# Three networks in one kernel: the last network's weights rebuilt from head 14 on, three of them as float16 pairs, and spatial weights 2.4 heads later

## The chip, the cores and the metric

The kernel runs on one core of a Trainium2 chip. Its metric is the device time in microseconds (us) of one execution; before the change it is 740.44 us, the median of three runs (739.67 to 742.71). A core has five engines with a queue each, worked in order: TensorE (PE, with a separate weight load PEld), VectorE (DVE), ScalarE (ACT), GpSimd (POOL), and SyncE (SP), which here only issues DMA transfers. An engine that waits for another holds up all that stands behind in its own queue.

## The reference

Three networks follow each other on float32 data with 4 batches, 576 tokens and 512 features (8 heads of 64 in the first).

```python
# 1: attention with a decay; heads are then put side by side: x[4, 576, 512]
scores = q @ k.T / 8 + cum[:, None] - cum[None, :]     # cum: cumulative sum of log(clip(f)), causal
x = softmax(scores) @ v
# 2: gated network with a product over the tokens
h = relu(x @ w_in); u, v = h[..., :512], h[..., 512:]
v_n = (v - mean(v)) / sqrt(var(v) + 1e-6)
x = (u * (w_spatial @ v_n + b_spatial)) @ w_out
# 3: last network; x_prev is x moved by one token
xk = mu_k * x + (1 - mu_k) * x_prev;  xr = mu_r * x + (1 - mu_r) * x_prev
out = sigmoid(xr @ w_r) * (relu(xk @ w_k) ** 2 @ w_v)
```

The kernel is handed float32 or, for the weights, float64 inputs: those arrive as pairs of 32-bit words, and the kernel rebuilds float32 numbers from the two words.

## The kernel before

**Products.** For precision every operand of a product is split into a high and a low half, and a product is three matmuls (high by high, high by low, low by high: table `T3`). In attention scores and in network 2 up to the gate the halves are float16 (`f16` in the profile); for `w_out`, and in all of network 3, they are `float32r`, a four-byte format (`f32` in the profile).

**Stages.** Attention goes head by head, 32 heads in all, 8 to a batch; a head's scores, row maxima (DVE, line 311), transposed scores, exponentials (ACT, line 339), causal zeros (POOL, line 344) and product with `v` (PE, line 357). When the 8 heads of a batch are done, the batch goes through network 2: `m1v` and `m1u` (the two halves of `x @ w_in`), a normalization (`ln1` to `ln4`), `m2` (the product over the tokens and the gate, written to DRAM as `gd`). Then tokens are cut into five chunks (four of 512, one of 256), and each chunk goes through `m3` (`gated @ w_out`), `mix` (xk and xr, split in halves) and `chunk`: `m4` (`xk @ w_k`), `m5` (the square times `w_v`), `m6` (`xr @ w_r`). The matmuls of `m3` to `m6` all have line 722.

**What sets the order.** `add` puts steps on a list, each with a time in heads (13.9: nine tenths into head 13) and a priority; `run` sorts them and emits their instructions. A scheduler then moves instructions, except those that `pin` keeps in the order of the program. Network 2 of a batch is planned from 2.7 heads after the batch's last head on, over 7 heads, and over 4 heads for the last batch (time 34.7 to 38.7), by which time attention is over.

**Weights.** A block of weights (128 rows, 512 columns, 512 KB raw) is fetched by SP into `wst` and rebuilt by `raw_convert`: one multiplication on ACT (line 97) and three integer operations on DVE (lines 100, 104, 105); `split` writes the halves, high on ACT (line 61) and low on DVE (line 62). `w_in` is rebuilt in the first heads, `w_spatial` by `weights_spatial`, which is planned from time 4.6 on (`P["wsp"]`) and ends in five transposing DMAs (line 491). The weights of `m3` to `m6` are fetched and rebuilt only when all attention heads have been emitted: `body` releases the attention buffers and then calls one block per 0.22 of a head between the steps of the last batch's network 2 (`w_out` 4 blocks, `w_k` 8, `w_r` 4); `w_v` (8 blocks) follows beside the first `m3`, the first `mix` and the first `chunk`.

**Buffers at the end.** PSUM and on-chip buffers of network 2 (`k.acts`, `k.w`) are released after its last step, and the buffers of `mix` and `chunk` (`k.p2`) take their place. So `mix` waits for the last write of `gd` out of `u`.

## Time and profile before

| what | us |
|---|---|
| median of three runs | 740.44 (739.67 to 742.71) |
| the profiled execution | 738.6 |
| its span, first to last instruction | 736.9 |
| PE busy in the span | 668.1 (91%) |
| DVE busy | 421.1 (57%) |
| ACT busy | 372.0 (50%) |

All durations of the sections below come from the one profiled execution, which has a span of 736.9 us and 1.7 us around it. In rows of the profile L357 is line 357 of the kernel before; `o<-e,v` means that tile `o` is written from tiles `e` and `v`; x12 counts instructions. Matmuls overlap in the engine, so a group's busy time is not a sum of durations, and the distance from one start to the next tells more than one matmul's length.

### The profile page before, as it was taken

The numbers are of one execution on the slowest core, as the hardware profiler recorded it, in microseconds if no ns is written. First come the engines' busy times: TensorE is split into PE (matmuls) and PEld (weight loads), VectorE is DVE, ScalarE is ACT, GpSimd is POOL, SyncE is SP. The second block draws the span as 40 slices with busy tenths as digits, with TensorE's granted clock in tenths as the row PEclk, the third lists the DMA queues.
The fourth block names the chain that finished last, engine by engine and source line by source line (L and its number), as shares of the span: only waits on it lengthen the run. The fifth ranks groups of instructions, "written<-read, shape, count | busy, mean of one in ns | idle before, by whom it ended". The sixth has DMA issues, their size and how long they took to land.

```text
span 736.9 us, 11024 instructions
## 1 busy us (share of the span) xinstructions
PE 668.1 (91%) x3718; PEld 495.8 (67%) x3718; DVE 421.1 (57%) x1147; ACT 372.0 (50%) x740; POOL 180.4 (24%) x385
## 2 busy tenths in 40 slices
PE   0368978999999999999997599999999999999997
PEld 0235645566775677657765477888888888888896
DVE  4987885684656744554029789886225422732342
ACT  4626886576445853356417359655235323632431
POOL 7023635554445444444322000000000000000000
PEclk9999979999999999999999899999999999999999
DMA  8997867676664333400035464531010100010010
GB/s 218 205 200 159 190 140 148 132 157 104 137 144 106 70 65 97 105 18 18 18 113 198 130 191 143 153 106 57 1 37 7 58 0 15 17 40 1 1 58 28
DMA packets 130681, 69.78 MB, mean 95 GB/s; under 512 B 114704, under 2 KB 115312, under 8 KB 130624
## 3 DMA queue, kind: packets, MB, share of 16 engines
q1 hardware_dynamic: 128032, 67.89, 37.8%
q10 hardware_dynamic: 2592, 1.19, 0.7%
q8 instruction: 29, 0.48, 0.3%
q14 instruction: 28, 0.23, 0.1%
HBM read 42.06 MB, written 9.79 MB: 70 GB/s over the span
## 4 chain that ended last, share of the span: by engine, by line
PE 71%; DMA 11%; DVE 8%; ACT 3%; POOL 3%; issue 2%; SPq 1%; ACTq 0%; DVEq 0%; POOLq 0%
PE m L722 38%; PE o L357 10%; PE t L335 5%; PE s L302 5%; PE m L583 5%; PE m1v L512 5%; PE m1u L566 4%; DMA qA<-md 1%; POOL x L396 1%; DMA wst<-in_moe_w_k_dram 1%; DVE junk L311 1%; POOL e L344 1%; DMA sr<-rd 1%; DMA u<-in_f_dram 1%; DMA gd<-u 1%
## 5 line engine op out<-in xcount | busy, mean ns | idle before, releaser
L357 PE MATMUL o<-e,v 128*128 128x320 f32 (+4 forms) x448 | 112.6, 379 | 4.5 <-POOL e L344 2.4
L722 PE MATMUL m<-xx,moe_w_k 128*128 128x512 f32 (+1 forms) x480 | 107.5, 373 | 0.4 <-ACT x L717 0.4
L722 PE MATMUL m<-moe_w_v,k 128*128 128x512 f32 x432 | 104.8, 391 | 0.0
L311 DVE CUSTOM_DVE_ANT_0 junk<-s,mask 128x512 bf16<-128x512 f32 (+4 forms) x160 | 76.0, 475 | 47.4 <-PE s L302 41.1
L722 PEld LDWEIGHTS m<-xx,moe_w_k 128*128 128x128 f32 x480 | 83.9, 188 | 18.2 <-ACT x L717 0.9
L339 ACT ACTIVATE e<-t,qa 128x512 f32<-128x512 f32 (+1 forms) x128 | 71.7, 591 | 45.2 <-PE t L335 44.5
L722 PEld LDWEIGHTS m<-moe_w_v,k 128*128 128x128 f32 x432 | 80.7, 188 | 17.7
L357 PEld LDWEIGHTS o<-e,v 128*128 128x128 f32 x448 | 77.0, 196 | 22.1 <-POOL e L344 5.8
L344 POOL TENSOR_SCALAR_AFFINE_SELECT e<-e 128x128 f32<-128x128 f32 (+1 forms) x160 | 52.8, 346 | 114.1 <-ACT e L339 107.3
L758 DVE TENSOR_TENSOR tmp<-tmp 128x512 f32<-128x512 f32 (+1 forms) x40 | 25.5, 638 | 88.0 <-ACT tmp L757 87.8
L302 PE MATMUL s<-kT,qT 128*128 128x512 f16 (+2 forms) x192 | 56.3, 301 | 19.6 <-DVE nm L311 10.9
L583 PE MATMUL m<-wspT,vn 128*128 128x288 f16 x384 | 55.7, 294 | 2.7 <-DVE u L586 2.7
L757 ACT ACTIVATE tmp<-m 128x512 f32<-128x512 f32 (+1 forms) x40 | 22.1, 556 | 71.3 <-PE m L722 71.1
L512 PE MATMUL m1v<-win,xt 128*128 128x512 f16 x240 | 57.4, 379 | 0.7 <-POOL xt L403 0.7
L566 PE MATMUL m1u<-xt,win 128*128 128x288 f16 x384 | 52.5, 286 | 4.6 <-ACT u L568 4.6
L302 PE MATMUL s<-kA,qA 67*128 67x512 f16 (+2 forms) x192 | 51.2, 303 | 5.0 <-DMA kA<-kT 3.7
L722 PE MATMUL m<-gh,moe_w_out 128*128 128x512 f32 (+1 forms) x240 | 53.8, 373 | 1.8 <-DVE u L586 1.1
L335 PE MATMUL t<-qA,kA 69*128 69x512 f16 (+2 forms) x192 | 50.5, 289 | 5.3 <-DMA qA<-md 4.3
L396 POOL TENSOR_TENSOR x<-xo,sr 64x576 f32<-64x576 f32 x32 | 45.4, 1417 | 23.4 <-DMA sr<-rd 22.2
L708 POOL COPY x<-x 128x4 f32<-128x4 f32 x4 | 1.2, 311 | 200.9 <-ACT x L717 200.9
L722 PE MATMUL m<-moe_w_r,xx 128*128 128x512 f32 x216 | 50.3, 392 | 0.0
L335 PE MATMUL t<-qT,kT 128*128 128x512 f16 (+2 forms) x192 | 49.9, 290 | 0.0
(159 smaller groups left out, 1067.8 us busy)
## 6 DMA issues: line engine op xcount, KB each, us to landing
sr<-rd SPq DMA_DIRECT2D x32, 144.0 KB
gd<-u SPq DMA_DIRECT2D x16, 288.0 KB
out_dram<-o SPq DMA_DIRECT2D x18, 256.0 KB
knat<-in_k_dram SPq DMA_DIRECT2D x32, 128.0 KB
v<-in_v_dram SPq DMA_DIRECT2D x32, 128.0 KB
g<-gd SPq DMA_DIRECT2D x16, 256.0 KB
wst<-in_moe_w_k_dram SPq DMA_DIRECT2D x8, 512.0 KB
wst<-in_moe_w_v_dram SPq DMA_DIRECT2D x8, 512.0 KB
```

The lines of the kernel that those rows point to most:

```text
L302: self.nc.tensor.matmul(s[:, o:o + n], self.tok(qn, p, h, 128 * ib - 64, 128)[0:r], self.tok(kn, p, h, k0, n)[0:r], start=(j == 0), stop=( ...
L311: self.nc.vector.tensor_tensor_reduce(out=self.junk[r0:, 0:n], in0=self.s[u % 2][r0:, o:o + n], in1=self.mask[r0:, m0:m0 + n], op0=ALU.add ...
L335: self.nc.tensor.matmul(t[:, o:o + n], self.tok(kn, p, h, 128 * c, 128)[0:r], self.tok(qn, p, h, q0, n)[0:r], start=(j == 0), stop=(j == 1))
L339: self.nc.scalar.activation(self.e[g][:, 512 * u:512 * u + n], t[:, 0:n], AF.Exp, scale=self.qa[p][:, 5:6])
L344: self.nc.gpsimd.affine_select(out=e, in_=e, pattern=[[1, n]], compare_op=ALU.is_ge, fill=0.0, base=0, channel_multiplier=-1)
L357: self.nc.tensor.matmul(o[:, 256 + f:256 + q1], v[:, c, h // 2, 64 * (h % 2):64 * (h % 2) + 128], e[:, off:off + q1 - f], start=(c == 0), ...
L396: self.held(p, self.nc.gpsimd.tensor_tensor(self.xp[r], self.xo.pop(2 * p + h)[r], self.sr[r], ALU.mult))
L512: nc.tensor.matmul(self.m1p, xt[:, xs, 128 * j:128 * j + 128], self.win[:, ws, kc, 512:1024], start=(kc == 0 and n == 0), stop=(kc == 3 an ...
L566: self.nc.tensor.matmul(o, self.win[:, ws, kc, fs], self.xt[(4 * b + kc) % 8][:, xs, ts_], start=(kc == 0 and n == 0), stop=(kc == 3 and n ...
L583: nc.tensor.matmul(o, pairs[n][0], pairs[n][1], start=(n == 0), stop=(n == 13))
L722: self.nc.tensor.matmul(out, l, r, start=(first and j == 0), stop=(last and j == len(pairs) - 1))
L758: nc.vector.tensor_tensor(tmp[:, 0:n], tmp[:, 0:n], tmp[:, 0:n], ALU.mult)
```

## The change

The diff, cut to its core. What is left out gives the same buffers other names and places: staging tiles become slices of one area (`area`), and the tiles of `k`, `q` and `v` are kept (`kept`) so that weights can be written into them when attention no longer reads them.

```diff
-         w1=-3.8, w0=1.0, wsp=4.6)
+         w1=-3.8, w0=1.0, wsp=7.0)
...
+            if k == "g" and x[1] and x[2]:
+                add(t + (0.5 if b < 3 else 0.2), 3, self.gsq, b, x[0])
+        add(s + length + (0.7 if b < 3 else 0.3), 3, self.gsum, b)
...
+    def gsq(self, b, fc):
...
+        self.pin(self.sumsq(self.ga[b][:, fc:fc + 1], self.u[:, fc], self.junka[:, 0:self.S]))
+    def gsum(self, b):
+        self.nc.vector.tensor_reduce(self.G[:, b:b + 1], self.total(self.ga[b], 4), AX.X, ALU.add)
...
+    def w2_conv(self, n):
+        e = self.e2[n] = self.we[n % 2 if n < 4 else (n - 4) % 3]
+        self.raw_convert(self.raws[n % 2], e, True)
+    def w2_sq(self, n):
+        self.pin(self.sumsq(self.am2[:, n:n + 1], self.e2[n], self.junka[:, 0:512]))
+    def w2_scale(self, n):
...
+            self.pin(nc.scalar.mul(self.w2[nm][kc][:, 0, c:c + 512], self.e2[m], s))
+    def w2_low(self, n):
...
+            self.pin(self.nc.vector.scalar_tensor_tensor(lo, self.e2.pop(m), self.rs[:, x:x + 1], hi, ALU.mult, ALU.subtract))
...
+    def plan_w2(self):
...
+        t = [13.9 + 1.5 * i for i in range(4)] + [25.2 + 0.75 * i for i in range(8)] + [31.2 + 0.55 * i for i in range(4)]
...
+        tv = [33.75 + 0.4 * i for i in range(8)]
...
     def m3(self, i):
...
-        gh = p.tile([128, 2, 4, 512], F32R, tag="gh", bufs=1, name="gh")
+        gh = self.gh
...
-            nc.scalar.copy(x2[:, m, 1:1 + n], ps[:, 0:n])
+            nc.scalar.mul(x2[:, m, 1:1 + n], ps[:, 0:n], gm[:, 1:2])
             yield
+        self.sumsq(self.st3[:, i:i + 1], x2[:, :, 1:1 + n], gh[:, 0, :, 0:n])
+        yield
+    def scale3(self, i):
...
+            nc.vector.tensor_reduce(sc[:, 0:1], self.total(self.st3[:, i - 1:i + 1], 2, self.ps3), AX.X, ALU.add)
...
     def mix(self, i, w):
-        xh = self.xx[w] = p.tile([128, 2, 4, 512], F32R, tag=f"xx{w}", bufs=1, name=f"xx{w}")
+        if w == 0:
+            self.scale3(i)
+        mu = self.scale4(i, w)
+        xh = self.xx[i, w] = (self.p2 if i % 2 else p).tile([128, 2, 4, 512], F16, tag=f"xx{w}", bufs=1, name=f"xx{w}")
...
+    k.plan_w2()
+    k.run(G + 1.45)
+    for p in (k.at, k.pso, k.pst, k.pss):
+        p.release()
+    k.phase3()
+    first = (x for y in (k.m3(0), k.m3(1), k.mix(0, 0), k.mix(0, 1)) for x in y)
     last = G + 1.45
     while k.steps:
-        last += 0.22
+        last += 0.25
         k.run(last)
-        next(w2, 0)
+        next(first, 0)
```

So `w_out`, `w_k` and `w_r` and what they are multiplied with become pairs of float16. Since float16 has a small range, each block of 128 weight rows, the gated `u` of each batch and `x2` of each chunk get a power of two as a scale, worked out from sums of squares (ACT), a sum over the partitions by a matmul with ones (`total`, `tot` in the profile) and a few operations on 1 to 8 columns (DVE). `w_v` and the squares stay `float32r`. The blocks are now steps of the list: `w_out` at times 13.9 to 18.4, `w_k` at 25.2 to 30.45, `w_r` at 31.2 to 32.85, `w_v` from 33.75 on. The loop over the last batch's network 2 calls pieces of `m3(0)`, `m3(1)` and `mix(0, ...)` instead of blocks of weights; `chunk(i)` calls pieces of `m3(i + 2)` and `mix(i + 1, ...)`.

On PE, where the last batch's network 2 ends, stood this before (`wspT` and `v_105` are `m2`'s operands, `gh,moe_w_out` is `m3`, `xx,moe_w_k` is `m4`):

```order
L583 LDWEIGHTS v_105
L583 MATMUL m_4889<-wspT,v_105 128x288
L722 MATMUL m_4943<-gh,moe_w_out 128x512 x12
L722 MATMUL m_4957<-gh,moe_w_out 128x512 x12
L722 MATMUL m_4971<-gh,moe_w_out 128x512 x12
L722 MATMUL m_4985<-gh,moe_w_out 128x512 x12
L722 MATMUL m_5071<-xx_4999,moe_w_k 128x512 x2
```

And at one place among the last batch's `m2` matmuls on PE stands this now (`w2k` and `w2r` hold `w_k`, `xx` is `mix`'s output, line 890 is `m3` to `m6`, line 596 is `m2`):

```order
L890 LDWEIGHTS w2k
L890 MATMUL m_5261<-xx_5048,w2k 128x512
L890 LDWEIGHTS w2r
L890 MATMUL m_5261<-xx_5048,w2r 128x512
L596 LDWEIGHTS vn
L596 MATMUL m_5146<-wspT,vn 128x288
```

Both pieces of `m3` and the first `m4` matmuls have moved ahead of the end of network 2.

On DVE, after seven eighths of the heads' row maxima (line 311, `junk<-s,mask`), stood this before, between a gate of `m2` (line 586) and the next:

```order
L586 SCALAR_TENSOR_TENSOR u<-m_3465,sw,u 128x288
L311 ISA junk,nm_159<-s,mask 128x512
L311 ISA nm_159 128x1
L323 CAST mr<-mrow 20x128
L311 ISA junk,nm_159<-s,mask 128x448
L311 ISA nm_159 128x1
L311 ISA junk,nm_159<-s,mask,nm_159 128x64
```

At the same place on DVE stands this now (`wstage_1819` holds raw and rebuilt weights, here of `w_k`):

```order
L599 SCALAR_TENSOR_TENSOR u<-m_3506,sw,u 128x288
L110 TENSOR_SCALAR wstage_1819<-wstage_1819 128x512
L114 SCALAR_TENSOR_TENSOR wstage_1819<-wstage_1819 128x512
L326 ISA junk,nm_155<-s,mask 128x512
L326 ISA nm_155 128x1
L115 SCALAR_TENSOR_TENSOR wstage_1819<-wstage_1819 128x512
L338 CAST mr<-mrow 20x128
L326 ISA junk,nm_155<-s,mask 128x448
```

The three operations of a block's rebuilding now stand between the row maxima of one head.

## Rows read from the trace of the kernel before

**Rows 1.** The page: its first line, busy time and share of each engine.

```profile
span 736.9 us, 11024 instructions
...
PE 668.1 (91%) x3718; PEld 495.8 (67%) x3718; DVE 421.1 (57%) x1147; ACT 372.0 (50%) x740; POOL 180.4 (24%) x385
```

**Rows 2.** Windows of 20 us: busy us of each engine, granted clock, DMA share.

```profile
100.00:120.00 20.00, 17.04 (x87) 11.24 (x87) 14.86 (x72) 13.67 (x31) 7.89 (x16) 0.77 0.67 136
120.00:140.00 20.00, 16.88 (x100) 10.49 (x98) 11.17 (x39) 11.69 (x22) 12.83 (x18) 1.00 0.66 140
320.00:340.00 20.00, 20.00 (x115) 11.83 (x114) 12.57 (x39) 11.98 (x27) 7.88 (x32) 1.00 0.06 16
360.00:380.00 20.00, 20.00 (x140) 14.22 (x138) 3.56 (x8) 3.01 (x6) 8.14 (x9) 1.00 0.15 46
400.00:420.00 20.00, 13.52 (x97) 9.75 (x96) 15.16 (x28) 9.17 (x19) 1.85 (x7) 0.91 0.47 153
```

**Rows 3.** Timeline of PE, last batch's network 2: start, us, what, [idle <-releaser].

```profile
388.52 3.10 PE L566 MATMUL m1u<-xt,win 128*128 128x288 f16 x24
...
413.21 1.14 PE L583 MATMUL m<-wspT,v 128*128 128x288 f16 x4 [4.70 <-DVE v L553]
...
431.29 11.46 PE L722 MATMUL m<-gh,moe_w_out 128*128 128x512 f32 x48 [1.13 <-DVE u L586]
442.60 3.89 PE L722 MATMUL m<-xx,moe_w_k 128*128 128x512 f32 x16
...
458.19 3.06 PE L722 MATMUL m<-xx,moe_w_k 128*128 128x512 f32 x12 [0.44 <-ACT x L717]
```

**Rows 4.** Timeline of PE, network 3, chunks of 512 tokens.

```profile
499.62 5.88 PE L722 MATMUL m<-moe_w_r,xx 128*128 128x512 f32 x25
505.34 5.65 PE L722 MATMUL m<-moe_w_v,k 128*128 128x512 f32 x24
510.83 5.76 PE L722 MATMUL m<-xx,moe_w_k 128*128 128x512 f32 x24
516.43 2.96 PE L722 MATMUL m<-gh,moe_w_out 128*128 128x512 f32 x12
```

**Rows 5.** Timeline of PE, network 3, the last chunk with 256 tokens.

```profile
716.20 1.58 PE L722 MATMUL m<-xx,moe_w_k 128*128 128x256 f32 x12
717.61 1.55 PE L722 MATMUL m<-moe_w_v,k 128*128 128x512 f32 x6
```

**Rows 6.** Timeline of PE, float16 matmuls with 512 columns.

```profile
149.36 2.75 PE L512 MATMUL m1v<-win,xt 128*128 128x512 f16 x12
151.95 0.70 PE L357 MATMUL o<-e,v 128*128 128x320 f32 x2
```

**Rows 7.** Timeline of PE, float16 matmuls with 288 columns.

```profile
268.32 2.37 PE L566 MATMUL m1u<-xt,win 128*128 128x288 f16 x18
270.52 0.30 PE L335 MATMUL t<-qA,kA 69*128 69x320 f16 x1
```

**Rows 8.** Lines of DVE, 340 to 460 us: busy us, mean ns, idle before.

```profile
L104 DVE SCALAR_TENSOR_TENSOR we<-we,wst 128x512 int32<-128x512 int32 x16 | 10.9, 684 | 0.1
...
L100 DVE TENSOR_SCALAR wst<-wst 128x512 int32<-128x512 int32 x17 | 7.2, 425 | 2.5 <-DMA wst<-in_moe_w_k_dram 1.6 <-DMA wst<-in_moe_w_out_dram 0.7
```

**Rows 9.** Lines of ACT, 340 to 460 us.

```profile
L97 ACT ACTIVATE we<-wst 128x512 f32<-128x512 f32 x17 | 11.4, 681 | 13.8 <-DMA wst<-in_moe_w_k_dram 12.6 <-DMA wst<-in_moe_w_out_dram 1.1
...
L61 ACT CAST moe_w_k<-we 128x512 fp32r<-128x512 f32 x8 | 4.9, 613 | 5.4 <-DVE we L105 5.4
```

**Rows 10.** Waits, whole span: us in total, times, longest us.

```profile
ACT e L339 <- PE t L335: 44.5, 37, 5.5
...
PE s L302 <- DVE nm L311: 10.9, 11, 3.3
```

**Rows 11.** Timeline of SP's issues: the weights' transposes.

```profile
114.06 2.94 SPq L491 DMA_TRANSPOSE wspT<-n  x2
```

**Rows 12.** Lines of PE by shape, whole span: a sum over the partitions.

```profile
L71 PE MATMUL tot<-qa,ones 128*128 128x2 f32 x32 | 5.9, 255 | 15.4 <-POOL xt L186 12.5 <-ACT junka L66 2.9
```

More of the change, by code (lines that the diff above doesn't have):

```diff
@@ L125, in setup @@
         self.kc = self.early[0:32, 1280:2240].bitcast(F16).rearrange("p (i c) -> p i c", i=3)
-        self.nat = {(nm, i): at.tile([128, 2, 5, 64], F32, name=f"{nm}nat{i}") for nm in "kq" for i in range(3)}
+        nat = self.kept("nat")
+        self.nat = {(nm, i): nat[:, 640 * (2 * i + n):640 * (2 * i + n + 1)].rearrange("p (h c d) -> p h c d", h=2, c=5) for n, nm in enumerate("kq") for i in range(3)}
         for i in range(2):
@@ L492, in weights_spatial @@
             yield
-        stp.release()
     def m1v(self, b, j, part):
@@ new lines, in w2_last, with w2_fetch @@
+    def w2_last(self):
+        t = self.kept("nat", "w2r")
+        self.w2["moe2_w_k"].append(t[:, 0:1024].bitcast(F16).rearrange("p (i c) -> p i c", i=2))
+        w = t[:, 1024:3072].bitcast(F16).rearrange("p (i k c) -> p i k c", i=2, k=4)
+        self.w2["moe2_w_r"] = [w[:, :, k] for k in range(4)]
+        self.g2 = t[:, 3072:3584]
+    def w2_fetch(self, n):
+        nm, kc, c = self.blocks[n]
+        self.raw_load(self.raws[n % 2], nm, slice(128 * kc, 128 * kc + 128), slice(c, c + 512), self.nc.sync)
@@ new lines, in w2_conv @@
+    def w2_conv(self, n):
[4 more added lines that the diff above has]
+    def w2_scale(self, n):
+        nc = self.nc
+        nm, kc, c = self.blocks[n]
+        x = {"moe_w_out": 0, "moe2_w_k": 4, "moe2_w_r": 8}[nm] + kc
+        s, ss = self.rs[:, x:x + 1], self.am2[:, n:n + 1]
+        if c:
+            self.pin(nc.vector.tensor_tensor(ss, ss, self.am2[:, n - 1:n], ALU.add))
+        o = s.bitcast(I32)
+        x = nc.vector.tensor_scalar(o, ss.bitcast(I32), 1, 0x7F800000, op0=ALU.logical_shift_right, op1=ALU.bitwise_and)
+        if not c:
+            self.pin(x)
+        nc.vector.tensor_scalar(o, o, -1.0, float((127 + 15 + 62 - 40) * 2 ** 23), op0=ALU.mult, op1=ALU.add)
+        for m in (n - 1, n) if c else (n,):
+            c = self.blocks[m][2]
+            self.pin(nc.scalar.mul(self.w2[nm][kc][:, 0, c:c + 512], self.e2[m], s))
@@ new lines, in w2_low, with w2_norm @@
+    def w2_low(self, n):
+        nm, kc, c = self.blocks[n]
+        x = {"moe_w_out": 0, "moe2_w_k": 4, "moe2_w_r": 8}[nm] + kc
+        for m in (n - 1, n) if c else (n,):
+            c = self.blocks[m][2]
+            hi, lo = (self.w2[nm][kc][:, i, c:c + 512] for i in range(2))
+            self.pin(self.nc.vector.scalar_tensor_tensor(lo, self.e2.pop(m), self.rs[:, x:x + 1], hi, ALU.mult, ALU.subtract))
+    def w2_norm(self, x):
+        nc = self.nc
+        r = self.ri[:, 4 * x:4 * x + 4]
+        self.inv2(r, self.rs[:, 4 * x:4 * x + 4])
+        if x:
+            nc.vector.tensor_tensor(self.span[:, 1, x - 1], self.span[:, 0, x - 1], r, ALU.mult)
+            for o in range(2):
+                nc.vector.tensor_tensor(self.mu[:, x - 1, o], self.mu[:, x - 1, o], r, ALU.mult)
+            r = self.span[:, 1, x - 1]
+        nc.scalar.activation(self.junka[:, 0:4], r, AF.Square, scale=2.0 ** -25, accum_out=self.nn[:, x:x + 1])
+        self.pow2(self.nn[:, 4 + x:5 + x], self.total(self.nn[:, x:x + 1], 1), 1e-20, 15)
@@ L698, in runs, with phase3 @@
             t += m
+    def phase3(self):
+        self.ps3 = self.pool("ps3", space=PSUM)
+        self.p3 = self.pool("phase3", side="right")
+        t = self.kept("v1", "g3")
+        self.gh = t[:, 0:2048].bitcast(F16).rearrange("p (i k c) -> p i k c", i=2, k=4)
+        self.g = [t[:, 2048 + 512 * i:2560 + 512 * i] for i in range(2)] + [self.g2]
+        self.gam = t[:, 3072:3136]
+        self.chunks = [(512 * i, min(512, 2304 - 512 * i)) for i in range(5)]
+        self.x2, self.xx = {}, {}
     def m3(self, i):
@@ L745, in chunk @@
         nc, p = self.nc, self.p2
+        sc = self.sc3[:, 8 * i:8 * i + 8]
         t0, n = self.chunks[i]
-        xk = self.xx[0]
-        wk, wr, wv = [self.w2["moe2_w_" + x] for x in "krv"]
+        xk = self.xx[i, 0]
+        wk, wr = [self.w2["moe2_w_" + x] for x in "kr"]
         J = n // 128
```

234 lines of the change are left out of this document (140 added, 94 removed).

## The prediction

> **What bounds the kernel now.** I read the page first, then windows of 20 us, then the timeline of PE where the windows show it idle, and last the timeline where it is full, to get its pace. The page has PE busy for 91% of the span and no other engine over 57% [rows 1]: PE is the bound wherever it doesn't wait, and a change is worth what it takes off PE's own time or off its waits. The windows show three kinds of stretch [rows 2]. Before about 140 us PE waits (17.04 and 16.88 of 20 us), with DVE and ACT half to three quarters full. Later, up to the end of attention, it is full (20.00 at 320 and at 360 us), and DVE and ACT are nearly idle at 360 (3.56 and 3.01). At 400 us, after attention, it waits most (13.52, at a granted clock of 0.91), while DVE is at 15.16: that is where weights are rebuilt.
>
> How much is lost there comes from the timeline [rows 3]. From 388.52 to 431.29 us, which is 42.77, PE does what is left of the last batch's network 2: 96 matmuls of `m1u` and 112 of `m2`, all with 288 columns. In a full stretch 18 of these take 268.32 to 270.52, 122.2 ns each [rows 7], so 208 are 25.4 us of work, and 17.4 are lost. The longest single gap, 4.70, is a wait for DVE's line 553, behind rebuilding in DVE's queue. `m3(0)`, 48 matmuls, takes 431.29 to 442.60; at the pace of network 3, found below, 11.1, so 0.2 lost. From 442.60 to 458.19 the rows (seven of them left out) list 60 matmuls, 13.8 of work in 15.59: 1.8 lost. Together 19.4 us. After that its starts follow each other evenly [rows 4].
>
> Its pace in network 3: 73 matmuls (25, 24, 24) from 499.62 to 516.43 are 230.3 ns each with 512 columns [rows 4]; with 256 columns 12 take 716.20 to 717.61, 117.5 each [rows 5]. In float16, 12 of 512 columns take 149.36 to 151.95, 215.8 each [rows 6].
>
> **Part 1: float16 for three weights.** Per chunk of 512 tokens `m3` has 48 matmuls, `m4` 96 and `m6` 48; four chunks and the 24 of the last chunk's `m6` make 792 with 512 columns. Each should fall from 230.3 to 215.8: 792 x 14.5 = 11.5 us. The last chunk's 144 with 256 columns should fall from 117.5 to 122.2 x 256 / 288 = 108.6: 1.3 us. I take 12.8. `m5` (432) stays. All of this lies on the path, since PE is full there. The bounds: 0, if the four-byte type is not what costs 14.5 ns, and 12.8.
>
> The Trainium skill speaks against this part: "TensorE: Matmul & The Clock Gate", "Step-by-step: what each phase is for", says that throughput is N cycles for N columns, one column a cycle, whatever the type. By that rule both types would pass at one pace and this term would be nothing; the rows above, 14.5 ns apart in one execution, don't bear it out for the four-byte type, and I go by them.
>
> **Part 2: the stretch after attention.** Sixteen blocks leave it, and `m3(0)`, `m3(1)` and the first `mix` enter, as does `w_v` (eight blocks). So PE has 96 matmuls of `m3` to put between network 2's, and the first `m4` matmuls stand among the last of `m2`. The 19.4 us can come back as far as nobody else is the bound. From the last row maximum to the first `m4` DVE's new queue holds 14 blocks (2.48 us each: one operation of 425 ns, three of 684 [rows 8]; 35 us) and 60 operations of `m3`, `mix`, the normalization and the gates (0.5 to 0.7 each, some 36 us) and some small ones: about 75. ACT's holds about as much: 14 blocks of a multiplication (681), a high half (613) [rows 9] and for six of them a sum of squares (I take 681), 22 us, and the rest of `m3`, `mix`, network 2 and the last exponentials, some 55. PE has about 22 us of the last heads, then 13.7 (`m2` of batch 2), 12.9 (`m1v`), 11.8 (`m1u`), 20.7 (two `m3`) and 5 (`m2`): 86. So PE is still the longest, with 10% to spare, in three queues that wait for each other. In that stretch DVE and ACT are nearly idle now for 20 us and more [rows 2], which is the room. I let a quarter of the loss stay, 5 us, and so take a gain of 14.5. Bounds: 19.4, and 0, where ACT and DVE hold PE up as now.
>
> **Part 3: rebuilding during attention.** Twelve blocks or so go into a stretch where PE is full. Added per block: DVE 2.48, ACT 1.98. Six stand between the row maxima of the last four heads, some 40 us, where DVE now has 12.57 of 20 [rows 2]: 15 us more make it nearly full there. What is behind a block's three DVE operations is the next row maximum, then the score that waits for its PSUM. The cover is that PE rarely waits for a row maximum: 10.9 us in the whole span [rows 10]. If the cover goes, each block costs up to its DVE time. ACT's exponentials, which `pv` needs, stand behind at most one more ACT operation, 0.68. I take 3 us; bounds 0 and 12 x 2.48 = 30, nearest to the row of waits.
>
> **Part 4: spatial weights later.** Their work (five transposes by SP, for example two in 2.94 us [rows 11], some 8 us of DVE and 10 of ACT) goes from about 95 to 120 us to about 120 to 150. The first stretch has DVE at 14.86 and a granted clock of 0.77, the second DVE at 11.17 and 1.00 [rows 2]; soon after, network 2 gives PE other work. The first need, `m2` of batch 0 at head 15, is far off. SP's transposes again stand between those of `q` and `k`. I take a gain of 2; bounds a gain of 6 and a loss of 4, the transposes' SP time at the new place.
>
> **Part 5: sums and scales.** Twelve sums over the partitions: 16 such sums now are 32 matmuls with a busy time of 5.9 us [rows 12], 0.37 each, so 4.4 at most; I take 3, bounds 0 and 4.4. The small DVE operations and the sums of squares stand beside a chunk's 48 us of PE and are ready a chunk ahead: nothing, and 2 us where the first chunk has no such lead (in part 2's remainder).
>
> **Sum.** Of the profiled execution's 738.6 us: - 12.8 - 14.5 + 3 - 2 + 3 = 715.3. The median shown, 740.44, is 1.8 above that execution, so I predict 717 us.
>
> **Rivals.**
> - *The stretch after attention stays as it is.* ACT (some 77 us) and DVE (75) become the bound beside PE's 86, and the waits on each other lose the 19.4 again. For: three queues within 10%. Against: their idle time at 360 us. Time: 717 + 14.5 = 731.
> - *The pace doesn't change.* A matmul goes by its columns, and the 14.5 ns come from the stretch, not from the type. Against: nothing else differs in the two rows that PE would feel, both at full clock. Time: 717 + 12.8 = 730. This is what the skill's rule above would make of it.
> - *All is hidden.* No remainder, no cost in attention, the spatial weights gain 5: 717 - 5 - 3 - 3 = 706, and the sums cost nothing, 703.
> - *Slower: attention waits for the rebuilding.* DVE's second operation of a block waits for ACT's multiplication, which stands behind an exponential that waits for PE, 1.2 us on average (44.5 over 37 [rows 10]); row maxima stand behind it, and scores behind them. If each of 12 blocks holds PE by 2.48 + 1.2 = 3.7, 44 us, the time is 717 - 3 + 44 = 758. It decides from 2.2 us a block, where the gains of 26 are used up. For: DVE full at 300 to 340 us. Against: the row of waits, and PE's queue has network 2 between its scores.
>
> **Chances.** The forecast 0.66, the first rival 0.12, the second 0.05, the third 0.13, the slower one 0.04. A measurement here can't tell less than 0.5% from no change, 736.7 to 744.1. Faster: 0.66 + 0.13 + 0.05 + 0.08 of the first rival, 0.92; no change: the rest of the first rival, where other costs come on top, 0.04; slower 0.04. The range that leaves out 2 in 10 goes from 704 (nearly all hidden) to 730 (the first two rivals at its edge).
>
> **What would show it.** Part 1: `m4` and `m6` at 216 ns from start to start in the timeline, `m5` at 230. Part 2: windows after attention with PE at 19 or more and the clock at 1.00; a wait of PE for ACT or DVE of more than 2 us there speaks for the first rival. Part 3: row maxima's and exponentials' waits on the PE rows between 200 and 340 us, against 10.9 now. Part 4: PE's busy time from 60 to 160 us. Wrong it would be above all if the last head ended later than now by 10 us or more, or if PE waited at the start of the first `m5`, whose squares need buffers that network 2 gives up last.

## The result, and the profile after

The changed kernel takes 728.71 us, the median of four runs (727.59 to 734.51), beside 740.06 of the kernel before on the same chip (739.41 to 742.71). The ratio is 0.986, with an interval of 0.983 to 0.989. The forecast was 717.0 with a range of 704 to 730: the direction is right and the time lies in the range, but 11.4 us were gained of 23 forecast. The profiled execution of the changed kernel takes 727.6 us, its span is 725.8.

The page after, its first line and the busy time of each engine; they answer to [rows 1].

```profile
span 725.8 us, 11269 instructions
...
PE 658.4 (91%) x3742; PEld 422.3 (58%) x3742; DVE 452.6 (62%) x1283; ACT 407.2 (56%) x820; POOL 193.4 (27%) x385
```

PE is 9.7 us less busy, and still busy for 91% of the span: its matmuls became faster, and its waits in sum did not become fewer. The windows of 20 us tell where, columns as in [rows 2].

```profile
100.00:120.00 20.00, 18.80 (x99) 12.58 (x98) 14.45 (x60) 13.76 (x30) 12.43 (x19) 0.78 0.67 134
120.00:140.00 20.00, 18.87 (x112) 11.52 (x111) 18.57 (x61) 13.40 (x28) 10.52 (x19) 1.00 0.72 134
...
320.00:340.00 20.00, 19.71 (x110) 11.09 (x109) 15.38 (x34) 12.78 (x29) 10.46 (x25) 1.00 0.22 72
340.00:360.00 20.00, 17.03 (x112) 12.66 (x111) 14.99 (x32) 15.12 (x32) 10.90 (x23) 0.91 0.23 69
360.00:380.00 20.00, 19.54 (x133) 14.06 (x132) 15.35 (x47) 14.06 (x31) 7.17 (x11) 1.00 0.43 136
400.00:420.00 20.00, 19.48 (x111) 10.78 (x110) 17.66 (x40) 15.51 (x33) 6.36 (x17) 1.00 0.47 147
420.00:440.00 20.00, 14.46 (x99) 9.40 (x97) 14.58 (x37) 15.13 (x28) 4.32 (x9) 1.00 0.27 79
```

The kernel before in the two windows that neither [rows 2] nor the prediction shows:

```profile
340.00:360.00 20.00, 20.00 (x147) 15.13 (x146) 1.95 (x5) 11.32 (x22) 7.06 (x15) 1.00 0.06 17
420.00:440.00 20.00, 16.63 (x87) 12.40 (x86) 16.03 (x29) 9.44 (x17) 0.00 (x0) 0.91 0.65 198
```

At 100 and 120 us PE has some 2 us more than before. At 360 us DVE and ACT, nearly idle before (3.56 and 3.01), are three quarters full. At 400 us PE is full where it had 13.52. But there are two holes: 340 to 360 us, in attention, where PE was full before, and 420 to 440 us, after it.

**How the waits are counted here.** For each stretch, the time from its first matmul's start to the next stretch's, less its matmuls at the full pace of the two formats: 216 ns for 512 columns in float16, 231 for `float32r`, fewer columns in proportion. (`pv` is slower than that in both kernels, 269 ns for 320 columns; that is in the waits of both.) In the table below, head 14 stands for the first transposed score product of that head, "last" for the last one of attention.

| PE's waits, us | before | after | change |
|---|---|---|---|
| start to head 8 | 65.8 | 63.8 | -2.0 |
| head 8 to 14 | 17.8 | 15.4 | -2.4 |
| head 14 to 20 | 10.6 | 16.3 | +5.7 |
| head 20 to 29 | 15.2 | 17.4 | +2.2 |
| head 29 to 30 | 2.4 | 7.8 | +5.4 |
| head 30 to last | 1.7 | 1.7 | 0 |
| last to end | 21.1 | 14.1 | -7.0 |
| sum | 134.6 | 136.5 | +1.9 |
| matmuls at full pace | 585.6 | 572.7 | -12.9 |

Together -11.0; the span fell by 11.1. The matmuls lost what was forecast; the waits gave nothing, because what went after attention came back within it. The first row is that execution's own: over all kernels below it lies between 63.1 and 69.4 without a pattern. How far the other rows scatter is told by kernels in which every engine has the same order up to head 25 or later. The changed kernel and two of those below have 16.3, 16.8 and 16.8 us in heads 14 to 20, and 15.4, 16.4 and 15.3 in heads 8 to 14; but two others (transfers by ACT's queue, below, without and with `w_v` apart) have 15.1 and 13.8, and 17.6 and 19.9. So from single profiles a difference of up to some 2.5 us in one stretch can be scatter, and +5.7 and +5.4 are well clear of it. Whole times of one kernel scatter by 3 to 9 us.

Part 1 is seen in PE's timeline in network 3 (start, us, what), which answers to [rows 4].

```profile
485.85 3.14 PE L890 MATMUL m<-moe_w_v,k 128*128 128x512 f32 x12
488.83 2.76 PE L890 MATMUL m<-g,wstage 128*128 128x512 f16 x12
491.43 2.10 PE L890 MATMUL m<-xx,w2k 128*128 128x512 f16 x9
493.37 0.81 PE L890 MATMUL m<-xx,w2r 128*128 128x512 f16 x3
493.83 3.14 PE L890 MATMUL m<-moe_w_v,k 128*128 128x512 f32 x12
```

(Matmuls of one product carry names of two weights where the records cut them; the format is what counts.) Between two groups of `m5`, 36 matmuls take 485.85 to 493.83, 7.98 us: 24 in float16 at 216 ns are 5.18, 12 in `float32r` at 231 are 2.77, and 0.03 is left. All 36 at the pace before would have taken 8.29.

The first hole, in attention, in PE's timeline:

```profile
343.91 0.25 PE L350 MATMUL t<-qT,kT 128*128 128x192 f16 x1
345.87 0.19 PE L350 MATMUL t<-qA,kA 69*128 69x64 f16 x1 [1.72 <-ACT e L354]
...
346.89 0.23 PE L336 MATMUL mrow<-ident,nmh 128*128 128x128 f16 x1 [0.79 <-DVE nmh L334]
347.58 3.54 PE L372 MATMUL o<-e,v 128*128 128x256 f32 x8 [0.47 <-ACT mv L545]
350.91 1.30 PE L579 MATMUL m1u<-xt,win 128*128 128x288 f16 x8
```

A transposed score waits for an exponential to free its PSUM, then the row maxima's matmul for DVE. The eight `pv` matmuls behind it take 3.33 us from start to start; by the medians of their line (216, 112 and 269 ns for 256, 128 and 320 columns) they would take 1.7. Windows of 1 us tell why, columns as above:

```profile
347.00:348.00 1.00, 0.54 (x3) 0.37 (x3) 0.28 (x1) 1.00 (x4) 0.48 (x3) 0.91 0.41 115
348.00:349.00 1.00, 1.00 (x5) 0.91 (x4) 0.67 (x3) 1.00 (x4) 0.45 (x3) 0.50 0.66 180
...
350.00:351.00 1.00, 1.00 (x4) 0.42 (x3) 0.97 (x2) 0.98 (x2) 1.00 (x1) 0.50 0.03 5
```

After the waits the granted clock is 0.50, the lower of its two levels (1.2 GHz), until 351 us: the hole costs 1.6 us more than its waits. ACT's timeline names what the exponential stood behind:

```profile
344.62 0.62 ACT L560 CAST vn<-vt 128x512 f16<-128x512 f32 x1 [0.72 <-DVE vt L555]
345.14 0.68 ACT L354 ACTIVATE e<-t,qa 128x512 f32<-128x512 f32 x1
```

Line 560 belongs to batch 2's normalization and waits for DVE's line 555, which comes after a block's lines 114 and 115 in DVE's queue and then waits itself for GpSimd's part of the normalization; that part follows DVE's line 541, which started at 341.63, right behind line 114 (340.93 to 341.71). The second hole, after attention, in PE's timeline and (second fence) ACT's:

```profile
419.27 3.24 PE L579 MATMUL m1u<-xt,win 128*128 128x288 f16 x24 [0.52 <-ACT u L581]
422.35 3.19 PE L890 MATMUL m<-g,wstage 128*128 128x512 f16 x14
427.43 2.56 PE L579 MATMUL m1u<-xt,win 128*128 128x288 f16 x18 [1.89 <-ACT u L581]
...
435.59 1.63 PE L579 MATMUL m1u<-xt,win 128*128 128x288 f16 x12 [1.45 <-ACT u L581]
439.01 1.63 PE L596 MATMUL m<-wspT,vn 128*128 128x288 f16 x12 [1.79 <-ACT u L581]
```

```profile
426.30 0.69 ACT L107 ACTIVATE wstage<-wstage 128x512 f32<-128x512 f32 x1 [1.28 <-DMA wstage<-in_moe_w_v_dram]
426.89 0.48 ACT L581 ACTIVATE u<-m1u,ds 128x288 f32<-128x288 f32 x1
...
433.88 0.69 ACT L107 ACTIVATE w2k<-wstage 128x512 f32<-128x512 f32 x1 [1.43 <-DMA wstage<-in_moe_w_v_dram]
```

PE waits for line 581, the relu of `m1u`, and that stands in ACT's queue behind a block of `w_v` that waits for its transfer.

### The profile page after: what moved, and what is told of

Same layout as the page of the kernel before. It is cut to its first block, busy times and chain, and to the rows that moved or that the text cites. A ratio compares the mean times of both kernels' runs of the same rounds, so it can differ in the third digit from the quotient of the medians.

```text
span 725.8 us, 11269 instructions
## 1 busy us (share of the span) xinstructions
PE 658.4 (91%) x3742; PEld 422.3 (58%) x3742; DVE 452.6 (62%) x1283; ACT 407.2 (56%) x820; POOL 193.4 (27%) x385
## 4 chain that ended last, share of the span: by engine, by line
PE 59%; DMA 12%; DVE 12%; ACT 6%; POOL 4%; issue 4%; SPq 2%; ACTq 0%; DVEq 0%; POOLq 0%
PE m L890 37%; PE o L372 6%; PE m L596 4%; PE t L350 3%; PE m1v L525 3%; PE s L317 3%; PE m1u L579 2%; DMA rd<-r 2%; DMA nat<-in_q_dram 2%; DMA qA<-md 2%; POOL x L411 1%; DVE junk L326 1%; ACT e L354 1%; DMA sr<-rd 1%; DMA qA<-qT 1%
## 5 line engine op out<-in xcount | busy, mean ns | idle before, releaser
L372 PE MATMUL o<-e,v 128*128 128x320 f32 (+4 forms) x448 | 116.5, 388 | 4.5 <-ACT xo L380 2.2
L890 PE MATMUL m<-moe_w_v,k 128*128 128x512 f32 x432 | 112.0, 409 | 0.0
L359 POOL TENSOR_SCALAR_AFFINE_SELECT e<-e 128x128 f32<-128x128 f32 (+1 forms) x160 | 55.7, 362 | 128.9 <-ACT e L354 121.1
L890 PE MATMUL m<-xx,w2k 128*128 128x512 f16 (+1 forms) x360 | 77.4, 358 | 0.0
L317 PE MATMUL s<-kT,qT 128*128 128x512 f16 (+2 forms) x192 | 55.9, 300 | 17.4 <-DVE nm L326 8.9
L930 ACT ACTIVATE tmp<-m,w2k 128x512 f32<-128x512 f32 (+1 forms) x40 | 25.8, 644 | 71.0 <-PE m L890 70.9
L411 POOL TENSOR_TENSOR x<-xo,sr 64x576 f32<-64x576 f32 x32 | 47.9, 1498 | 28.5 <-DMA sr<-rd 27.3
L890 PEld LDWEIGHTS <-w2k 128*128 128x128 f16 x360 | 34.0, 98 | 35.0 <-issue 4.4
L890 PE MATMUL m<-g,wstage 128*128 128x512 f16 (+1 forms) x240 | 51.2, 358 | 0.0
L579 PEld LDWEIGHTS <-win 128*128 128x128 f16 x384 | 37.2, 99 | 18.5 <-issue 8.3
L890 PE MATMUL m<-w2r,xx 128*128 128x512 f16 x216 | 47.4, 379 | 0.0
```

What stands on the lines that cost most here:

```text
L317: self.nc.tensor.matmul(s[:, o:o + n], self.tok(qn, p, h, 128 * ib - 64, 128)[0:r], self.tok(kn, p, h, k0, n)[0:r], start=(j == 0), stop=( ...
L359: self.nc.gpsimd.affine_select(out=e, in_=e, pattern=[[1, n]], compare_op=ALU.is_ge, fill=0.0, base=0, channel_multiplier=-1)
L372: self.nc.tensor.matmul(o[:, 256 + f:256 + q1], v[:, c, h // 2, 64 * (h % 2):64 * (h % 2) + 128], e[:, off:off + q1 - f], start=(c == 0), ...
L411: self.held(p, self.nc.gpsimd.tensor_tensor(self.xp[r], self.xo.pop(2 * p + h)[r], self.sr[r], ALU.mult))
L579: self.nc.tensor.matmul(o, self.win[:, ws, kc, fs], self.xt[(4 * b + kc) % 8][:, xs, ts_], start=(kc == 0 and n == 0), stop=(kc == 3 and n ...
L890: self.nc.tensor.matmul(out, l, r, start=(first and j == 0), stop=(last and j == len(pairs) - 1))
```

## The experiments

The tables give PE's waits by the stretches above. Each time is a median beside the kernel before on the same chip (739.5 to 741.0), with the ratio and its interval.

**The spatial weights alone.**

```diff
-         w1=-3.8, w0=1.0, wsp=7.0)
+         w1=-3.8, w0=1.0, wsp=4.6)
```

> The changed kernel with part 4 alone undone (spatial weights at 4.6 again). Waits here are PE's time in a stretch less its matmuls at their full pace. From the start of the trace to the first score product of head 14 they are 83.6 us in the kernel before and 79.3 in the changed one. Theory: these 4.3 us are part 4's, so they come back: 82 to 84 up to head 14 and a time of 731 to 733. Rival: the gain there comes from something else that changed with it (buffers of the early weights), the waits stay at 79 and the time at 728 to 729.

Measured: 736.1 us (0.993, 0.989 to 0.997), 3 more than expected, from runs between 730.4 and 739.1; the profiled execution took 731.2. Heads 8 to 14 have 17.8 us again, head 14 to last 41.7. The same edit the other way round, in the kernel before:

> The kernel before with part 4 alone: spatial weights at 7.0. Theory: it gains 2.4 us between heads 8 and 14 (17.8 to about 15.4), and as the scheduler's order of later heads changes with it, some of that is lost again from head 14 on (29.9 us before, 31 to 36 with it): 738 to 743. Rival: the order is not what costs; the gain stands alone and the waits from head 14 on stay at 30: 737 to 738.

Measured: 738.0 (0.996, 0.994 to 0.998); 14.9 us in heads 8 to 14, 31.5 from head 14 to last. So part 4 gains 2.4 to 2.9 us where it was forecast: heads 8 to 14 have 17.8 us in both kernels with 4.6, and 14.9 to 16.4 in the seven with 7.0 in which nothing else is changed before head 13. The 1.6 us more from head 14 on are within the scatter.

**The rebuilding in attention left out**, twice: with a transfer per block, and without any.

```diff
+        if n < 12:                                   # first
+            self.nc.sync.dma_start(self.w2[nm][kc][:, :, c:c + 512], self.fill...)
+            return
```

```diff
+            if n < 12:                                   # second
+                add(t[n], 7, self.w2_fill, n)    # gpsimd.memset
+                continue
```

> The changed kernel without the rebuilding of the first 12 blocks of the last network's weights (four of w_out, eight of w_k): a constant is copied from DRAM into their place (one transfer of SP per block as before, half the bytes), so ACT's and DVE's operations for them are left out and the output is not the reference's. From head 14's to the last score product PE's waits are 29.9 us before and 43.2 in the changed kernel. Theory: the 13.3 more are the price of rebuilding in attention; without it they are about 30 and the time is about 715. Rival: they come from the other order of work (sums of squares of the gates, spatial weights, transfers), the waits stay at 40 or more and the time at 725 to 729.

> The changed kernel in which the first 12 blocks cost neither ACT, DVE nor a transfer: GpSimd fills their place with a constant, at the same times in the plan (their rebuilding is left out, so the output is not the reference's). Without the rebuilding but with a transfer per block the waits from head 14 to the last score product stayed at 43.2 us. Theory: the transfers cost there (SP's queue, or the DMA engines in which the short transfers between a pair's row maxima and its second score product stand behind 256 or 512 KB): without them 30 to 34 us and a time of 714 to 720. Rival: neither work nor transfers of the rebuilding cost in heads 14 to 28; something else of the change does: 38 us or more, of which heads 14 to 20 have 16 to 17 as in the changed kernel, and a time of 721 to 727.

| PE's waits, us | after | with transfer | without |
|---|---|---|---|
| head 8 to 14 | 15.4 | 17.3 | 21.4 |
| head 14 to 20 | 16.3 | 17.4 | 18.1 |
| head 20 to 29 | 17.4 | 21.5 | 18.0 |
| head 29 to 30 | 7.8 | 2.6 | 2.6 |
| time | 728.7 | 727.7 (0.984, 0.981 to 0.988) | 729.5 (0.986, 0.981 to 0.990) |

The theory that the blocks' work or transfers cost 13 us falls. What stands in for the blocks is not free and not where it was planned: without transfers GpSimd's fillings, 0.95 us each, ran at 136 to 141 us, in heads 10 and 11, and at 298 to 311 us, where the scheduler had put them, so a part of the 21.4 us in heads 8 to 14 can be theirs. But heads 14 to 20 (181 to 250 us there) have no block, no transfer and no filling, and still 18.1 us of waits: there it can't be the rebuilding that PE waits for. One place bears the theory out, heads 29 to 30, where the window without the work is full again:

```profile
340.00:360.00 20.00, 20.00 (x138) 14.24 (x137) 8.43 (x28) 12.23 (x27) 9.41 (x28) 1.00 0.06 17
```

against 17.03 at a clock of 0.91. Elsewhere nothing came back: with the blocks gone the scheduler orders the rest in another way from about head 10 on, and PE waits at other places.

**Transfers by ACT's queue; no sums of squares of the gates.**

```diff
-slice(c, c + 512), self.nc.sync)
+slice(c, c + 512), self.nc.scalar if n < 12 else self.nc.sync)
```

> The changed kernel with the transfers of the first 12 blocks issued by ACT instead of SP. Theory SP: they hold up the loads, transposes and short transfers of q and k in SP's queue; so the waits from head 14 on fall from 43.2 to 36 to 40 us, the time to 721 to 726. Theory DMA: it is the engines' time, not the issue: 42 to 45 us and 727 to 731.

Measured: 727.6 (0.983, 0.980 to 0.987); 40.2 us from head 14 to last: between what the two theories expect, and no gain in the time. Heads 29 to 30 fall to 4.1, but 30 to last rises from 1.7 to 4.4, and heads 8 to 14 from 15.4 to 17.6.

```diff
-            if k == "g" and x[1] and x[2]:
-                add(t + (0.5 if b < 3 else 0.2), 3, self.gsq, b, x[0])
-        add(s + length + (0.7 if b < 3 else 0.3), 3, self.gsum, b)
```

> The changed kernel without the sums of squares of the gates: 16 operations of ACT with 576 columns, held in program order behind DVE's gates, and their four sums over partitions; a constant takes their place, so the scale of network 2's output is not the reference's. Theory: ACT stands there until DVE's gate is done, with exponentials behind it, in heads 15 to 18 and 23 to 26: the waits of heads 14 to 20 fall from 16.3 to 11 to 13, those from 20 to 29 from 17.4 to 15 or 16, and the time to 721 to 724. Rival: they are hidden: 16 to 17 and 17 to 18, 727 to 729.

Measured: 725.9 (0.980, 0.976 to 0.984). Heads 14 to 20 17.7, 20 to 29 15.1, last to end 12.2 (14.1 in the changed kernel): the stretch named stayed; the others have some 2 us less each, which is within the scatter.

**All three parts out of attention at once**, and a kernel before with its plan moved a little.

```diff
-wsp=7.0)
+wsp=4.6)
...      and the edits above: GpSimd's filling for the first 12 blocks, no gsq, no gsum
```

> The changed kernel with everything of the change taken out of heads 4 to 28 but the places of buffers: spatial weights at 4.6, no sums of squares of the gates, and the first 12 blocks neither fetched nor rebuilt, GpSimd filling them with a constant (so the output is not the reference's). What is left different from the kernel before in attention is the order into which the scheduler puts the same work, from about head 10 on. Theory: it is this order that costs: from head 14 to the last score product 36 to 42 us of PE's waits, as with single parts taken out, and a time of 724 to 730. Rival: each of the three parts alone is enough to cause the waits, and without all of them they are those of the kernel before: 29 to 32 us, and 714 to 719.

Measured: 725.7 (0.981, 0.978 to 0.985). From head 14 to last 35.1 us, between the two; the time is in the theory's range. Heads 14 to 20 fall to 11.5 and heads 29 to 30 to 2.6, nearly those of the kernel before (10.6 and 2.4), while heads 20 to 29, where GpSimd does eight of the fillings (296 to 308 us), stand at 19.4. The other four fillings ran at 127 to 131 us, and heads 8 to 14 have 20.7 us (17.8 before). So from head 8 to the last score product 55.8 us are left, 47.7 before and 58.6 in the changed kernel: the run shows that heads 14 to 20 can be had without the waits, and does not tell the order's share from that of the parts taken out.

```diff
-mlp=2.7,
+mlp=2.8,
```

> The kernel before with one number of the plan moved a little: network 2 of every batch starts 2.8 heads after the batch's last head and not 2.7. No work is added, removed or made longer; the scheduler orders it differently from head 9 on. Theory: the order before is a good one among many, and a small move of the plan costs as much as the change lost in attention: the waits from head 14 to the last score product rise from 29.9 to 35 to 42 us, the time to 744 to 752. Rival: the order matters little: 28 to 33 us and 739 to 742, and what the changed kernel loses there has a cause in its own work.

Measured: 741.2 (1.002, 1.000 to 1.004), 29.6 us from head 14 to last, 24.3 after it (21.1). For this move of the plan the theory falls: attention lost nothing by it. That no other order costs is not shown.

**The steps of a block further apart; blocks at other heads.**

```diff
+                add(t[n] + 0.25, 7, self.w2_conv2, n)    # DVE's part of the conversion
-            add(t[n] + 0.35, 7, self.w2_sq, n)
+            add(t[n] + (0.35 if n > 11 else 0.6), 7, self.w2_sq, n)
...      and the block's later steps likewise
```

> The changed kernel with the same work for the first 12 blocks, but the steps of a block that pass from ACT to DVE and back further apart in the plan (0, 0.25, 0.6, 0.95, 1.35 heads after its start in place of 0, 0, 0.35, 0.55, 0.8). Theory: what costs is that an operation at the head of ACT's or DVE's queue waits for the other engine's step of the same block, with exponentials and row maxima behind it; further apart they find each other done: PE's waits from head 14 on fall from 43.2 to 33 to 37 us, and the time to 719 to 723. Rival: what costs is the amount of work on DVE and ACT; it is the same here, so 42 to 44 and 728 to 729.

(In it the low half of one block of `w_k` is computed from numbers of `w_r`, which have taken its buffer by then.) Measured: 739.2 (0.998, 0.996 to 1.001), 47.7 us from head 14 to last and 18.8 after. The hand-over theory falls: with looser steps these waits are 4.5 us more, not less. The time is above both expectations, and the rival's amount of work does not explain the rise either.

```diff
-        t = [13.9 + 1.5 * i for i in range(4)] + [25.2 + 0.75 * i for i in range(8)] + ...
+        t = [20.5 + 0.7 * i for i in range(4)] + [25.2, 25.75, 26.3, 26.85, 29.4, 29.95, 30.5, 31.05] + ...
...      and tv at 0.62 for 0.4
```

> The changed kernel with w_v's blocks 0.62 heads apart, and the other blocks where network 2 leaves DVE most room: w_out at heads 20.5 to 22.6 (between the normalization and the gates of batch 1) in place of 13.9 to 18.4, w_k half before 27 and half from 29.4 on, so that none falls into the normalization of batch 2 (27.5 to 29.2), w_r at 31.6 to 33.1. Theory: a block costs where DVE's and ACT's queues hold network 2's own work: heads 29 to 30 fall from 7.8 us of waits to 3, heads 14 to 20 from 16.3 to 11 to 13, and with w_v apart (4.4 us in the stretch after) the time is 714 to 719. Rival: heads 14 to 20 stay at 16 (the cause there is another), or the waits reappear at the new places: 720 to 725.

Measured: 736.7 (0.995, 0.993 to 0.997). Heads 29 to 30 fall to 3.8, but heads 14 to 20 keep 16.5 with no block in them, and 20 to 29, where four went, rise to 26.1. The rival holds for the waits: they stay, and others appear at the new places. The time is 12 us above what either expected.

**Blocks of `w_v` further apart.**

```diff
-        tv = [33.75 + 0.4 * i for i in range(8)]
+        tv = [33.75 + 0.62 * i for i in range(8)]
```

> The changed kernel with the eight blocks of w_v 0.62 heads apart in the plan, not 0.40. After the last score product PE's waits are 12.1 us in the changed kernel (21.0 before), and 9.7 of them lie between the first matmul of m3 and the 97th, where ACT stands four times at a conversion of w_v that waits for its fetch, 3.6 us after SP could issue it. Theory: with the blocks further apart the fetches are in time, the waits of that stretch fall to 4 to 6 and the time to 723 to 725. Rival: ACT and DVE have too much to do there, whatever the order: 9 to 11 us stay and the time is 728 to 729; or w_v is then late for the first m5, and the time is above 730.

Measured: 725.6 (0.980, 0.977 to 0.982). Last to end 9.7 instead of 14.1; between the first matmul of `m3` and the 97th 5.3 instead of 9.7. PE's timeline there:

```profile
419.70 2.75 PE L890 MATMUL m<-g,wstage 128*128 128x512 f16 x12
422.36 3.10 PE L579 MATMUL m1u<-xt,win 128*128 128x288 f16 x24
425.29 2.75 PE L890 MATMUL m<-g,wstage 128*128 128x512 f16 x12
427.97 1.63 PE L579 MATMUL m1u<-xt,win 128*128 128x288 f16 x12
...
431.86 0.90 PE L579 MATMUL m1u<-xt,win 128*128 128x288 f16 x6 [1.83 <-ACT u L581]
...
438.64 1.63 PE L596 MATMUL m<-wspT,vn 128*128 128x288 f16 x12 [0.35 <-ACT u L581]
```

Of the waits for line 581, 6.0 us in the changed kernel, 2.2 are left, and ACT's waits for `w_v`, 3.9 us in four in the changed kernel, are gone. The theory stands. The wait of 1.83 us that is left has another cause: ACT's line 557 stood 2.11 us for DVE's line 555, which came behind a block's lines 114 and 115 and GpSimd's part of the normalization, as in the first hole. With that, the blocks of `w_k` outside of batch 2's normalization:

```diff
-[25.2 + 0.75 * i for i in range(8)]
+[25.2, 25.7, 26.2, 26.7, 27.2, 29.3, 29.9, 30.5]
```

> The changed kernel with w_v's blocks 0.62 heads apart and the eight blocks of w_k at 25.2, 25.7, 26.2, 26.7, 27.2, 29.3, 29.9 and 30.5, so that none is planned inside the normalization of batch 2 (27.5 to 29.2); up to head 25 the scheduler's order is that with w_v apart alone (725.6). Theory: at heads 29 to 30 it is the blocks in the normalization that cost, because DVE's and ACT's queues then hold the exponentials and row maxima up: 7.7 us of waits there become 2 to 4, and the time is 720 to 723. Rival: they cost wherever they are: the sum of the waits from head 24 to the last score product stays at 20, 725 to 727.

Measured: 728.0 (0.983, 0.980 to 0.987), its runs from 722.4 to 731.4. Heads 29 to 30 fall from 7.7 to 5.1, the waits from head 14 to last from 43.7 to 41.3: that points to place as a part of the hole, not all of it, as the 3.8 of the case before does, though 2.6 us is hardly beyond the scatter. In the whole time that gain doesn't show. And `w_v` apart with the transfers on ACT's queue:

> The changed kernel with two changes that helped or did no harm alone: w_v's blocks 0.62 heads apart and the first 12 transfers issued by ACT. If they add up: waits after the last score product 9 to 10 us, from head 14 to it 38 to 40, and a time of 721 to 724. If the gain of the second was only another order: 724 to 728.

Measured: 726.2 (0.983, 0.979 to 0.986): 39.5 us of waits from head 14, 10.8 after the last, near the first case; the time is the second's.

**GpSimd's operations in thirds.** The traces had shown something that the prediction left out: operations of DVE that end only after one of GpSimd's has ended. DVE's timeline and (second fence) GpSimd's in the changed kernel:

```profile
213.74 1.09 DVE L334 TENSOR_TENSOR nmh<-nm,nmh 128x10 f16<-128x10 f32 x1
...
322.35 1.92 DVE L114 SCALAR_TENSOR_TENSOR wstage<-wstage 128x512 int32<-128x512 int32 x1
...
325.75 0.72 DVE L115 SCALAR_TENSOR_TENSOR wstage<-wstage 128x512 int32<-128x512 int32 x1
```

```profile
213.04 1.77 POOL L303 TENSOR_SCALAR qA<-kA,qa 3x1280 f16<-3x1280 f16 x1
...
322.33 3.21 POOL L411 TENSOR_TENSOR x<-xo,sr 64x576 f32<-64x576 f32 x2
```

Line 334 takes 0.17 us elsewhere, and at 213.74 PE's `mrow` waits for it; line 114 takes 0.69. From head 14 to last 15 operations of DVE take 14.0 us more than the median of their kind (each over 250 ns more), 3 and 2.8 us in the kernel before. All 15 began while an instruction of GpSimd of 1.3 to 1.9 us ran and ended 0.01 to 0.55 us after the end of one. The Trainium skill has the rule: "SBUF — State Buffer", "SBUF: two separate sides", says that GpSimd and a DVE operation with two inputs in SBUF, or in a mode that uses two ports, share a pair of ports, which one of them holds for its whole instruction. The trace agrees in so far as ten of the 15 have two inputs; the other five (lines 110 and 555) have one, and no run here shows their mode. Row maxima, whose scores come from PSUM, ran 15 times wholly inside such an instruction of GpSimd without being longer than elsewhere.

```diff
-            self.held(p, self.nc.gpsimd.tensor_tensor(self.xp[r], self.xo.pop(2 * p + h)[r], self.sr[r], ALU.mult))
+            for c in range(0, 576, 192):     # and so for lines 303 and 418
+                self.held(p, self.nc.gpsimd.tensor_tensor(self.xp[r, c:c + 192], xo[r, c:c + 192], ...))
```

> The changed kernel with GpSimd's three long operations of a pair of heads (x from xo, the low half of x, a row of qA: 1.3 to 1.9 us each) cut into three pieces of a third each; the work is the same. In the changed kernel 15 operations of DVE between head 14 and the last score product take 1.1 to 1.9 us in place of 0.2 to 0.75 and end when such an operation of GpSimd does: 14.0 us, against 3 and 2.8 us in the kernel before. Theory port: DVE is shut out until GpSimd's instruction is done; with short ones it waits less: the excess falls to 3 to 7 us, PE's waits there from 43.2 to 34 to 39, and the time to 720 to 725. Rival: DVE's longer operations are not on PE's path: the excess falls and the waits stay at 41 to 45, 727 to 730. Or more pieces only mean more collisions: the excess stays at 12 or more.

Measured: 734.8 (0.993, 0.991 to 0.996). The excess falls to 4.9 us as expected, PE's waits for `nmh` from head 14 on from 3.1 to 0.8 (over the whole span they are 3.1 in both, as others appear earlier), but the waits from head 14 to last are 44.3 and heads 8 to 14 rise to 21.0: a third of line 411 takes 0.68 us, not 0.50, and causal zeros now stand behind more of them (PE waits 2.3 us for line 360, 0.3 before the edit). The time is above what was expected either way. So the collisions are there, and taking most of them away did not bring the 13 us back; as the edit also adds work to GpSimd, what they cost by themselves stays open. Together with `w_v` apart (735.0, 0.993, above both expectations), in the kernel before (741.6, 1.002) and with line 411 moved to DVE instead:

> Both at once: GpSimd's operations in thirds and w_v's blocks 0.62 heads apart. If the two gains add up: 716 to 721. If the thirds bring nothing: 724 to 727, as with w_v apart alone (725.6).

> The kernel before with GpSimd's three operations in thirds. Theory port: little to gain there, since only 3 of DVE's operations are shut out (2.8 us): waits from head 14 on 28 to 31 us, 738 to 741. If it gains as much as the changed kernel does with the same edit, the edit works by something else than the rebuilding's collisions.

> The changed kernel with w_v apart, and the longest of GpSimd's operations (x from xo, 32 with 64 rows and 576 columns, 1.50 us each) moved to DVE. Theory port: DVE has 32 more operations of some 0.75 us, 24 us in 360, but far fewer to wait for: the excess falls to 4 to 8 us, and the time is 720 to 726. Rival: DVE has no room for 24 us more, whatever the port does: waits of 46 or more, 729 to 735.

The last measured 727.5 (0.984, 0.981 to 0.986), excess 5.1 us, 40.6 from head 14 to last, but 22.6 in heads 8 to 14: no gain over `w_v` apart alone. In the kernel before, with the thirds, the waits from head 14 on are 3.9 us more and those of heads 8 to 14 are 3.4 less (14.4), and the time is the same.

## Why the prediction was wrong

By its own steps, forecast and measured (differences of the profiled executions):

| step | forecast | measured |
|---|---|---|
| part 1, pace | -12.8 | -11.0 (-12.9, and 1.9 given back) |
| part 2, after attention | -14.5 | -8.9 (21.1 to 14.1 holds the 1.9 of part 1) |
| part 3, attention from head 14 on | +3 | +13.3 (5.2 shown to be the rebuilding) |
| part 4, spatial weights | -2 | -2.4 |
| part 5, sums | +3 | about 0, not measured apart |
| start to head 8 | 0 | -2.0 (that execution's own) |

- **The step that failed is part 3.** "The cover is that PE rarely waits for a row maximum" was the reason for 3 of a possible 30 us, with a row of the whole span behind it [rows 10]. That row says nothing of this stretch: its 10.9 us all lie before head 8. From head 14 to the last score product PE waited for no row maximum before the change, and for 0.4 us after it; "against 10.9 now" between 200 and 340 us was a misreading. PE's waits from head 14 to the last score product, before (first fence) and after:

```profile
PE t L335 <- DMA qA<-md: 3.6, 3, 1.5
```

```profile
PE t L350 <- DMA qA<-md: 3.6, 3, 1.8
PE mrow L336 <- DVE nmh L334: 3.1, 3, 1.8
PE t L350 <- ACT e L354: 1.7, 1, 1.7
PE o L372 <- ACT mv L545: 0.5, 1, 0.5
PE s L317 <- DVE nm L326: 0.4, 1, 0.4
```

  What came are waits at links behind the maxima and at an exponential's PSUM: `mrow`, the matmul on the row maxima, waits for `nmh`, their halves (1.8 and 0.6 us of it where line 334 collided with GpSimd, 0.8 in the hole), a transposed score for an exponential. From `mrow` to the first transposed score, which needs `mrow`'s result over two transfers (`qA`), pairs 8 to 15 (heads 16 to 31) take 8.05 us on average, 6.97 before, but PE's wait at the end of it is 3.6 us in both. The list holds 6.6 of the 13.3 us, the lower clock in the hole 1.6; where the rest lies is not told apart.

  By cause: 5.2 us, in heads 29 to 30, are the rebuilding beside batch 2's normalization, shown by its absence in three runs. The 5.7 us in heads 14 to 20 are not the rebuilding alone (18.1 us with no block there); with the gates' sums and the moved spatial weights out as well they fell to 11.5, in another order. What each costs there, and what the order costs, stays open; the 2.2 us in heads 20 to 29 are within the scatter. So the rebuilding's own shown price is 5 us beside 3, and the other 8 of the 13.3 belong to no term: the prediction has none for the gates' sums of squares in ACT's queue and none for the new order of everything else in attention, and gives no reason for that. The slower rival (3.7 us a block, 44 in all) had the kind of cause right, queues that wait for each other, but not the chain (in the hole an exponential stands behind the normalization's line 560, not a row maximum behind a block), and its size wrong by three.
- **Part 2** had the direction and the sign of its doubt: of 21.0 us of waits 12.1 stayed beside 5 forecast. The count of three queues "with 10% to spare" left out that all blocks share two buffers for what is fetched and that a transfer, which waits for its buffer, takes 3.6 us from issue to conversion (422.71 to 426.30): ACT's queue stood for transfers, not for work. With the blocks apart, 7.7 of the 12.1 stay. Rival 1 is thus half right: its waits are there (1.9 us for ACT, just under its mark of 2), and one that is left with the blocks apart (1.83) is ACT waiting for DVE; the 4.4 us that went were a wait for transfers, which it did not have.
- **Part 1** came as forecast but for 1.9 us. The rival that the pace goes by columns alone is out: at full clock 216 and 231 ns stand side by side in one timeline. What the sum left out are small losses in a chunk with two formats, 1.9 us in all: the last matmul of `m5` takes 238 ns and the first in float16 after it 226, some 17 ns a round and 0.6 in 33 rounds; `m5` itself has a median of 232; the rest is not told apart.
- **Part 4** came out in size and place (2.4 to 2.9 us in heads 8 to 14). **Part 5** shows no cost of its own in the stretches; no run took its sums over partitions out in network 3.
- What "would show it wrong", a last head 10 us later, came nearly true: the last score product is at 366.6, 6.8 us later than before, though head 14 begins 1.2 earlier. That the time still lies in the range is owed to its width.

The best version that leaves no work out is the changed kernel with `w_v`'s blocks 0.62 heads apart: 0.980 (0.977 to 0.982) of the kernel before, beside 0.986 (0.983 to 0.989).

## What to carry to other kernels

Work put under a full engine costs by the chain that feeds it, link by link (maxima, sums, transfers, buffers), not by the one wait that the profile lists first; price it by walking that chain, with the waits of that stretch alone: a row over the whole span can lie entirely elsewhere, as the 10.9 us did here. A block with a transfer and two buffers wants its distance in the plan from the transfer's time, and an operation that waits for a transfer is a stop for all behind it. Where a scheduler orders the work, taking one cost out does not give its price back, and a stand-in is moved too: read the price by stretch, look where the stand-in ran, take the costs out together as well as singly, and learn the scatter from runs with the same order.
